# Two channel-weight pieces loaded behind the last pair's rows and staged where token sums will stand, in a one-core attention and token/channel-mixing kernel

## The chip, the core and the metric

The kernel runs on one core of one Trainium2 chip. The metric is the device time of one execution in microseconds (us). Three runs of the kernel before stand for it: 558.23, 559.42 and 561.3 us, median 559.42. The other figures come from one more execution, taken by the hardware profiler.

## What is computed

All data are float32. The reference first runs a decaying linear attention and then a token mixer and a channel mixer on its output:

```python
batch, n_heads, seq, head_dim = (4, 8, 768, 64)      # attention, in blocks of 64 rows
intra = (q k^T * Dmask) v                            # inside a block
inter = (q * lam_pow) kv_state                       # from the blocks before
x = attn_out.transpose(0, 2, 1, 3).reshape(4, 768, 512)
h = relu(x^T @ w_tok1) @ w_tok2                      # w_tok1 768x256, w_tok2 256x768
u = x + h^T
h2 = relu(u @ w_ch1) @ w_ch2                         # w_ch1 512x1536, w_ch2 1536x512
out = u + h2
```

## The kernel before

**Stages.** Attention works on 16 pairs of heads, `pairs[i] = (b, p)`, four pairs to each of the four batches. One loop over `i` from -2 to 15 (the first part of the span) computes the scores of pair i+1, the outputs of pair i, and between them pieces of the token mixer of batches already finished. The token pieces are taken from the list `groups`: `token_hidden` (18 matmuls of 256 columns into a tile `ph`, eighteen for each of four pieces of a batch) and `token_out` (6 matmuls of 384 columns into a tile `pu`, eight pieces of a batch). Batch 3's token outputs come behind the loop, in pairs of pieces. Then the channel mixer runs, in six groups of weights and four batches, with a seven-product scheme; it takes the rest of the span.

**The order is written by hand.** Each engine runs its queue in program order. The numbers in `take` say how many pieces of `groups` stage i runs, and `held` moves five of them: places 33 to 37 of the list become two hidden pieces of batch 3 (places 36 and 37) and then three output pieces of batch 2 (33 to 35). Stage 14 takes three pieces, stage 15 takes one, and four are left behind the loop. Smaller steps stand in `waiting`, and `later(n)` runs the next n of them between pieces.

**Loads.** `load_kq(i + 4)` at stage i loads a pair's rows: `kn`, four DMAs of 96 KB for `qn`, and from pair 8 on four of 96 KB for `kr` (L118). Runs of 32 numbers make their packets small. VectorE then turns `qn` and `kr` in blocks into `qT` (L255) and `kT` (L259), which the scores need. SP issues all of these loads in one queue.

**The first group's channel weights.** Their four raw pieces of 512 KB (i = 0 to 3 in `load_piece`) come in as 64-bit words. Each piece is narrowed to 32-bit floats by one step on ScalarE (L494) and four on VectorE (L495, L498, L501, L504), and then split into a high part (ScalarE, L486) and a low part (GpSimd, L487). All of that is staged in `w3`, which is the memory of batch 3's attention output, `uT[3]`. This has to be free before pair 12 writes there, so `later(99)` at stage 11 empties the list. Pieces 2 and 3 (`w_ch2` rows, L640) are issued by SP in stages 7 and 9, between the loads of pairs 11 and 12 and of pairs 13 and 14, and are narrowed in stages 10 and 11.

**Names.** `xp` is a transposed piece of the output of a pair (TensorE, L468); ScalarE rounds it to `xhi` (L475) and VectorE writes the rest, `xlo` (L476). `turn_back(i, 0)` and `turn_back(i, 1)` do this for the halves of pair i. L603 on VectorE adds a `pu` to `uT` and frees its bank; L565 and L566 finish a `ph`. L420 copies outputs from PSUM to `uT` (ScalarE). L333 masks scores and L303 scans states (VectorE); L316 and L282 are GpSimd's copies of states and its scaling of q. `first` holds steps that prepare batch 0's operands for the channel mixer (`t1` to `t4` are L698 and L731 on VectorE, `T1` to `T4` a cast L706 on ScalarE and a subtraction L711 on VectorE). `B11` and `B21` are two such operands whose low parts GpSimd makes.

**Banks.** `bank("sh", ...)` has three PSUM banks in turn and borrows the one of tag `xT` once a stage. The pieces `pu`, `ph` and `xp` all use them, so TensorE may be only three or four pieces ahead of what VectorE and ScalarE have emptied.

Of the kernel before, what the change touches and what calls it, by code (L numbers as in the profile page):

```python
# [13 lines left out]
U32 = mybir.dt.uint32  # L14
# [8 lines left out]
def kernel(  # L23
# [25 lines left out]
    DM = H * D  # L49
    FT = w_tok1.shape[1]  # L50
    FC = w_ch1.shape[1]
    P = 128
# [5 lines left out]
    SB = S // 2  # L58
# [5 lines left out]
    waiting = deque()  # L64

    def later(n):
        n += len(waiting) > (5 if len(groups) > 16 else 99)
        for _ in range(min(n, len(waiting))):
            waiting.popleft()()
# [6 lines left out]
    up = ctx.enter_context(tc.tile_pool(name="up", bufs=1))  # L76
# [14 lines left out]
    hidp = ctx.enter_context(tc.tile_pool(name="hidp", bufs=1, side="right"))  # L91
# [132 lines left out]
    n = 1  # L224
# [407 lines left out]
    def load_piece(g, i, raw):  # L632
        if i < 2:
            src = c1u[2 * i * P : 2 * (i + 1) * P, g * FG * 2 : (g + 1) * FG * 2]
            nc.sync.dma_start(
                out=raw.rearrange("p (t f) -> p t f", t=2), in_=src.rearrange("(t p) f -> p t f", p=P)
            )
        else:
            r0 = g * FG + (i - 2) * P
            nc.sync.dma_start(out=raw, in_=c2u[r0 : r0 + P, :])  # L640

    def narrow_piece(raw, a, sg):
        return narrow(raw.rearrange("p (n two) -> p n two", two=2), a, sg)
# [22 lines left out]
    def split_c2(to, i, a):  # L666
        c2h, c2l = to[4:]
        return lambda: split(c2h[:, i - 2], c2l[:, i - 2], a.bitcast(F32))
# [65 lines left out]
    weights = {}  # L734
# [10 lines left out]
    LATE = 7  # L745
    late_turns = deque([turn_q, turn_kr])
    idle = [lambda: None]
    held = [groups[n] for n in (36, 37, 33, 34, 35)]
    for n, f in enumerate(held):
        groups[33 + n] = f  # L750

# [1 line left out]
    for i in range(-2, NI):  # L755
        if 0 <= i + 1 < NI:
            pair = scores(i + 1)
            scale_q(i + 1)
        if i >= 0:
            outputs(i, 0)  # L760
        place = state(i + 1) if 0 <= i + 1 < NI else None
        if i + 1 in SCAN_FIRST:
            mask_scores(i + 1, 1, pair)
        work = [groups.popleft() for _ in range(take.get(i, 0))]
        if i == NI - 1:
            work.pop(0)()
        if i >= 0:
            outputs(i, 1)
            spare.append("xT")
        if i + 2 < NI and i != LATE:  # L770
            turn_q(i + 2)
            if i + 2 >= NKD:
                turn_kr(i + 2)
        if i + 2 < NI:
            if 0 < i + 2 < NP:
                masks(i + 2)
            turns = [(turn_k, 0), (turn_k, 1)] if i + 2 < NKD else []
            if i + 2 < NQ:
                turns += [(turn_q_rows, 0), (turn_q_rows, 1)]
            if i == -2:  # L780
                turns.sort(key=lambda x: x[1])
            for f, g in turns:
                f(i + 2, g)
        if place:
            place()
        later(0 if i == NI - 1 else 1 if work else 2)
        n = early.get(i, len(work) // 4)
        cuts = [0, n, max(n, (3 * len(work) + 1) // 4 if len(work) > 2 else len(work) // 2), len(work)]
        for n in range(3):
            for f in work[cuts[n] : cuts[n + 1]]:  # L790
                f()
                if i == LATE and n == 1 and late_turns:
                    late_turns.popleft()(i + 2)
                later(2 if len(work) < 3 else 1)
            if n < 2 and i >= 0:
                turn_back(i, n)
                later(1 if work else 2 + n)
            if n == 0 and i + 2 < NI:
                scale_k(i + 2)
                if i == LATE:  # L800
                    late_turns.popleft()(i + 2)
        if NSKIP - 4 <= i < NSKIP:
            own_blocks(i % 4)
        if NSKIP <= i + 2 < NI:
            load_firsts(i + 2)
        if i == -1:
            load_w1(0)
        if 0 <= i + 3 < NI and i >= -1:
            load_v(i + 3)
        if i == -1:  # L810
            load_w1(1)
        if i + 4 < NI:
            load_kq(i + 4)
        if i == -1:
            load_w1(2)
        if i == 3:
            load_w2()
        if 0 <= i < 3:
            convert_w1(i)
        if i == 5:  # L820
            weights[0] = group_tiles(0, False)
            w3 = words(3)
            load_piece(0, 0, w3[:, 2048:3072])
        if i == 4:
            steps = [w2_steps(n) for n in range(3)]
            waiting.extend(2 * idle + steps[0][:5] + idle + steps[0][5:] + steps[1][:2] + idle)
        if i == 5:
            waiting.extend(steps[1][2:5] + idle + steps[2][:2] + idle + steps[1][5:] + steps[2][2:] + idle)
        if i == 6:
            waiting.append(lambda: load_piece(0, 1, w3[:, 1024:2048]))  # L830
            steps = narrow_piece(w3[:, 2048:3072], w3[:, 0:512], w3[:, 512:1024])
            waiting.extend(idle + steps[:1] + 2 * idle + steps[1:2] + 2 * idle + steps[2:])
        if i == 7:
            steps = narrow_piece(w3[:, 1024:2048], w3[:, 512:1024], w3[:, 2048:2560])
            waiting.extend(3 * idle + steps)
            waiting.append(lambda: load_piece(0, 2, w3[:, 2048:3072]))
        if i == 8:
            waiting.extend(split_c1(weights[0], w3[:, 0:512], w3[:, 512:1024], nc.gpsimd))
        if i == 9:
            waiting.append(lambda: load_piece(0, 3, w3[:, 1024:2048]))  # L840
            waiting.extend(narrow_piece(w3[:, 2048:3072], w3[:, 0:512], w3[:, 512:1024]))
            waiting.append(split_c2(weights[0], 2, w3[:, 0:512]))
        if i == 10:
            homes[0] = {"B11": (up, None, 1), "B21": (up, None, 1), "T2": (kp, "kn", 2), "T1": (kp, "qn", 2)}
            homes[0] |= {"B22": (kp, "kr", 2), "T3": (kp, "kT", 2), "T4": (kp, "qT", 2)}
            first = build(0, 0, on_vector=("T1", "T2", "T3", "T4", "B22"))
            waiting.extend([first["B11"], first["B21"]])
            waiting.extend(narrow_piece(w3[:, 1024:2048], w3[:, 2048:2560], w3[:, 2560:3072]))
            waiting.append(split_c2(weights[0], 3, w3[:, 2048:2560]))
        if i == 11:  # L850
            later(99)
        if i == 13:
            for xs in (("t1",), ("t2", "T1.h"), ("T2.h", "T1.l"), ("T2.l", "t3", "t4"), ("T3.h", "T4.h"), ("T3.l", "T4.l")):
                waiting.append(lambda xs=xs: [first[x]() for x in xs])
    later(99)
    att.close()
    ch = ctx.enter_context(tc.tile_pool(name="ch", bufs=1, reuse_waits="tile"))
# [612 lines left out]
```

## Time and profile before

| | |
|---|---|
| runs: lowest, median, highest | 558.23, 559.42, 561.3 us |
| the profiled execution: its own time | 555.34 us |
| its span (first to last instruction) | 553.5 us |
| TensorE clock granted, share of full speed | 0.999 |
| busy share of TensorE, VectorE, ScalarE, GpSimd | 97%, 79%, 45%, 51% |
| bytes moved by DMA | 67.63 MB, mean 122 GB/s |
| loop over pairs with its token pieces | to about 166 us of the span |
| token outputs of batch 3 | 170.89 to 179.2 us |
| channel mixer | from 179.2 us |

The busy share of TensorE is a mean over stages; an idle interval shows only where a matmul starts later than the modelled end of the one before. Times inside the span are counted from its start. An interval of idle time in front of an instruction is given in square brackets in the timeline, with the engine and tile that ended it.

### The profile page before, as it was taken

The page shows a single profiled execution, that of the slowest core. Times are in us where ns is not written, and L with a number is a line of the kernel's source. Part 1 is how long each engine was busy: PE and PEld are TensorE (multiplying, and loading weights), DVE is VectorE, ACT ScalarE, POOL GpSimd, SP SyncE. Part 2 cuts the span into 40 slices and gives each one's busy share as a digit, 9 for nine tenths or more (in the row PEclk, how much of TensorE's full clock was granted, in tenths as well). Part 3 has the DMA queues.
Part 4 walks back from the last instruction along what each step waited for, and adds up shares of the span by engine and source line. Part 5 has one row for each costly group of instructions (what it writes and reads, how often), then busy time and mean ns, then how long its engine had stood idle before and what let it go on. Part 6 is the DMA issues. An engine that isn't in the chain of part 4 may idle for free.

```text
span 553.5 us, 11983 instructions
## 1 busy us (share of the span) xinstructions
PE 537.3 (97%) x4756; PEld 523.6 (95%) x4756; DVE 435.2 (79%) x657; ACT 247.4 (45%) x499; POOL 283.3 (51%) x260
## 2 busy tenths in 40 slices
PE   5999999979999999999999999999999999999997
PEld 4889999879889999999999999999999999999996
DVE  4787799668697989887878878788787878788894
ACT  3464543425252554343444443443455555445431
POOL 5667552737214464444435444354476656568550
PEclk9999999999999999999999999999999999999999
DMA  9999999999502534361725400014874131220276
GB/s 183 249 204 184 228 184 179 177 187 176 102 2 91 184 108 134 89 234 38 248 78 176 147 1 0 1 27 61 192 145 149 57 116 58 86 104 2 30 151 125
DMA packets 178760, 67.63 MB, mean 122 GB/s; under 512 B 166673, under 2 KB 168977, under 8 KB 178705
## 3 DMA queue, kind: packets, MB, share of 16 engines
q1 hardware_dynamic: 173472, 65.69, 49.5%
q10 hardware_dynamic: 5232, 1.18, 1.0%
q8 instruction: 37, 0.61, 0.4%
q14 instruction: 19, 0.15, 0.1%
HBM read 50.07 MB, written 16.78 MB: 121 GB/s over the span
## 4 chain that ended last, share of the span: by engine, by line
PE 81%; DMA 5%; SPq 5%; DVE 5%; ACT 1%; issue 1%; ACTq 0%; DVEq 0%
PE po L1149 22%; PE pa L923 13%; PE pc L923 9%; PE pb L923 7%; PE pa L1123 7%; PE pc L1123 5%; SPq L118 5%; DMA kr<-in_k_dram 3%; PE pd L923 3%; PE ph L561 2%; PE sc L371 2%; DMA qn<-in_q_dram 2%; PE pu L581 2%; PE xT L436 1%; PE pu L598 1%
## 5 line engine op out<-in xcount | busy, mean ns | idle before, releaser
L1162 DVE TENSOR_TENSOR uT<-po,uT 128x768 f32<-128x768 f32 x57 | 54.2, 952 | 16.5 <-PE po L1149 16.2
L938 ACT ACTIVATE c<-c 128x384 f32<-128x384 f32 x42 | 22.1, 526 | 58.5 <-DVE c L983 33.5
L316 POOL COPY stb<-sv 64x320 f32<-64x320 f32 x32 | 26.8, 839 | 35.1 <-DVE sv L303 34.1
L1129 DVE TENSOR_TENSOR uT<-pa,uT 128x768 f32<-128x768 f32 x36 | 34.4, 954 | 10.5 <-PE pa L1123 9.8
L940 POOL TENSOR_TENSOR h22l<-c,h22h 128x384 fp32r<-128x384 f32 x14 | 14.4, 1032 | 41.6 <-ACT h22h L939 41.6
L1129 DVE TENSOR_TENSOR uT<-pc,uT 128x768 f32<-128x768 f32 x27 | 25.8, 955 | 11.6 <-PE pc L1123 11.6
L487 POOL TENSOR_TENSOR c1l<-cs,c1h 128x512 fp32r<-128x512 f32 x15 | 19.3, 1296 | 23.2 <-ACT c1h L486 23.2
L333 DVE TENSOR_TENSOR a<-sc,mask 128x768 f32<-128x768 f32 (+1 forms) x32 | 25.9, 849 | 4.6 <-PE sc L371 4.1
L1149 PE MATMUL po<-h12h,c 128*128 128x384 f32 x112 | 28.7, 337 | 0.0
L1149 PE MATMUL po<-h11h,c 128*128 128x384 f32 x112 | 28.7, 337 | 0.0
L1149 PE MATMUL po<-h22h,c 128*128 128x384 f32 x112 | 28.6, 336 | 0.0
L1149 PE MATMUL po<-h21h,c 128*128 128x384 f32 x112 | 28.6, 336 | 0.0
L561 PE MATMUL ph<-xhi,w1h 128*128 128x256 f32 x96 | 28.2, 293 | 0.4 <-DVE uT L603 0.4
L561 PE MATMUL ph<-xhi,w1l 128*128 128x256 f32 x96 | 27.1, 283 | 0.0
L561 PE MATMUL ph<-xlo,w1h 128*128 128x256 f32 x96 | 27.1, 283 | 0.0
L282 POOL TENSOR_TENSOR qs<-qT,lamp 128x640 f32<-128x640 f32 x16 | 25.2, 1577 | 0.7 <-DVE qT L255 0.2
L476 DVE TENSOR_TENSOR xlo<-xp,xhi 128x384 fp32r<-128x384 f32 x32 | 17.7, 552 | 9.5 <-ACT xhi L475 9.4
L487 POOL TENSOR_TENSOR c<-cs,c 128x512 fp32r<-128x512 f32 x10 | 12.9, 1293 | 19.7 <-ACT c L486 19.7
L940 POOL TENSOR_TENSOR h21l<-c,h21h 128x384 fp32r<-128x384 f32 x14 | 17.7, 1262 | 8.8 <-POOL h22l L940 3.9
L940 POOL TENSOR_TENSOR h12l<-c,h12h 128x384 fp32r<-128x384 f32 x14 | 14.4, 1031 | 14.5 <-issue 10.4
L486 ACT CAST c1h<-cs 128x512 fp32r<-128x512 f32 x15 | 9.3, 617 | 26.7 <-DVE cs L660 18.9
L1149 PEld LDWEIGHTS po<-h12h,c 128*128 128x128 f32 x112 | 20.4, 188 | 0.0
(409 smaller groups left out, 2008.0 us busy)
## 6 DMA issues: line engine op xcount, KB each, us to landing
raw<-in_moe_w_ch_dram SPq DMA_DIRECT2D x20, 512.0 KB, 3.7
vn<-in_v_dram SPq DMA_DIRECT2D x16, 384.0 KB, 5.4
out_dram<-y SPq DMA_DIRECT2D x104, 48.0 KB, 1.9
qn<-in_q_dram SPq DMA_DIRECT2D x44, 96.0 KB, 3.6
kn<-in_k_dram SPq DMA_DIRECT2D x8, 384.0 KB, 6.6
kr<-in_k_dram SPq DMA_DIRECT2D x32, 96.0 KB, 3.1
dc1h<-c1h SPq DMA_DIRECT2D x4, 768.0 KB, 5.3
dc1l<-c1l SPq DMA_DIRECT2D x4, 768.0 KB, 6.7
```

Source lines behind the costliest of these rows:

```text
L118: nc.sync.dma_start(out=to[n * 32 : (n + 1) * 32].rearrange("p (blk d) -> p blk d", d=32), in_=sv[di])
L282: nc.gpsimd.tensor_mul(out=qss[i], in0=qTs[i][:, P:].rearrange("p (c i) -> p c i", i=P), in1=lamp[:, p, None, :].broadcast_to([P, NC - 1, P]),
L316: nc.gpsimd.tensor_copy(out=st[r, :, h, :], in_=sv[r].rearrange("p (e c) -> p c e", c=NC - 1))
L333: nc.vector.tensor_mul(out=a, in0=pair.rearrange("p h (c i) -> p h c i", i=w), in1=mask[:, 2 * p : 2 * p + 2, None, ms].broadcast_to([P, 2 ...
L487: nc.gpsimd.tensor_sub(out=lo, in0=src, in1=hi.bitcast(F32))
L561: nc.tensor.matmul(out=ph, lhsT=w[:, c, fs], rhs=x[:, c], start=(i == 0), stop=(i == 3 * NC - 1))
L923: nc.tensor.matmul(out=to, lhsT=w[:, t], rhs=x[:, t], start=(start and i == 0), stop=(i == 5), skip_group_check=not start,)
L940: nc.gpsimd.tensor_sub(out=hl, in0=src, in1=hh.bitcast(F32))
L1123: nc.tensor.matmul(out=pair[x][:, t], lhsT=w[:, t], rhs=h, start=(start and i == 0), stop=(i == 2), skip_group_check=not start,)
L1129: nc.vector.tensor_add(out=ub, in0=pair[x], in1=ub)
L1149: nc.tensor.matmul(out=to, lhsT=w[:, jj, t * P : (t + 1) * P], rhs=h, start=(i == 0), stop=(i == 3 * JG - 1))
L1162: nc.vector.tensor_add(out=ub, in0=po, in1=ub)
```

## The change

Pieces 2 and 3 are no longer loaded in stages 7 and 9 into `w3`. They go into a new tile `raw2`, in the place that the token sums (`hid`) of batches 1 and 3 share (tag `h1`), with `up`'s tiles for `B21` as temporaries. SP issues them in stages 11 and 12, the first behind the rows of pair 15. Their narrowing moves from stages 10 and 11 to stages 13 and 14; in stage 14 each step runs in front of a step of `first`. `B21` is prepared last, since its memory is the temporary. `held` is gone: the last pieces of `groups` are in their plain order, since batch 3's hidden pieces now need the memory of `raw2`.

```diff
     idle = [lambda: None]
-    held = [groups[n] for n in (36, 37, 33, 34, 35)]
-    for n, f in enumerate(held):
-        groups[33 + n] = f
+
+    def second_steps(n):
+        return narrow_piece(raw2[:, n], temp2[0], temp2[1]) + [split_c2(weights[0], n + 2, temp2[0])]
...
         if i == 7:
             steps = narrow_piece(w3[:, 1024:2048], w3[:, 512:1024], w3[:, 2048:2560])
             waiting.extend(3 * idle + steps)
-            waiting.append(lambda: load_piece(0, 2, w3[:, 2048:3072]))
...
-        if i == 9:
-            waiting.append(lambda: load_piece(0, 3, w3[:, 1024:2048]))
-            waiting.extend(narrow_piece(w3[:, 2048:3072], w3[:, 0:512], w3[:, 512:1024]))
-            waiting.append(split_c2(weights[0], 2, w3[:, 0:512]))
         if i == 10:
...
-            waiting.extend([first["B11"], first["B21"]])
-            waiting.extend(narrow_piece(w3[:, 1024:2048], w3[:, 2048:2560], w3[:, 2560:3072]))
-            waiting.append(split_c2(weights[0], 3, w3[:, 2048:2560]))
+            waiting.append(first["B11"])
         if i == 11:
             later(99)
+            raw2 = hidp.tile([P, 2, 1024], U32, tag="h1", name="raw2")
+            temp2 = [up.tile([P, 2 * SB], U32, tag=f"B21{x}0", name=f"temp2{x}")[:, 0:DM] for x in "hl"]
+        if i in (11, 12):
+            load_piece(0, i - 9, raw2[:, i - 11])
+        if i == 12:
+            waiting.extend(idle + second_steps(0))
         if i == 13:
-            for xs in (("t1",), ("t2", "T1.h"), ("T2.h", "T1.l"), ("T2.l", "t3", "t4"), ("T3.h", "T4.h"), ("T3.l", "T4.l")):
-                waiting.append(lambda xs=xs: [first[x]() for x in xs])
+            xss = (("t1",), ("t2", "T1.h"), ("T2.h", "T1.l"), ("T2.l", "t3", "t4"), ("T3.h", "T4.h"), ("T3.l", "T4.l"))
+            for f, xs in zip(second_steps(1), xss):
+                waiting.append(lambda f=f, xs=xs: [f()] + [first[x]() for x in xs])
+            waiting.append(first["B21"])
```

On SP's queue, the end of the loads in the loop. Before, from the rows of pair 14 on (`kr_1695` is pair 14's, `kr_2068` pair 15's):

```order
L118 DMA kr_1695<-in_k_dram 32x24x32 x4
L640 DMA uT_63<-in_moe_w_ch_dram 128x1024
L182 DMA vf_1866<-in_v_dram 64x6x64
...
L118 DMA kr_2068<-in_k_dram 32x24x32 x4
L182 DMA vf_2233<-in_v_dram 64x6x64
L168 DMA vn_2235<-in_v_dram 128x12x64
L182 DMA vf_2385<-in_v_dram 64x6x64
```

Now, from the rows of pair 15 on:

```order
L118 DMA kr_2048<-in_k_dram 32x24x32 x4
L640 DMA raw_2053<-in_moe_w_ch_dram 128x1024
L182 DMA vf_2217<-in_v_dram 64x6x64
L168 DMA vn_2219<-in_v_dram 128x12x64
L640 DMA raw_2053<-in_moe_w_ch_dram 128x1024
L182 DMA vf_2377<-in_v_dram 64x6x64
```

Both pieces now stand behind the last `kr`, and between them the v rows of pairs 14 and 15. The same holds for the earlier piece, which stood behind the `kr` of pair 11.

On ScalarE's queue in stage 13, before, from the copies of pair 13's outputs on:

```order
L420 COPY uT_63<-xT_2282 128x3x128
L475 CAST xhi_2174<-xp_2346 128x3x128
L275 ACTIVATE kd_2352<-kn_2061,mask 128x320 x2
L475 CAST xhi_2174<-xp_2371 128x3x128
L420 COPY uT_63<-xT_2431 128x3x128
```

Now:

```order
L420 COPY uT_63<-xT_2267 128x3x128
L494 ACTIVATE temp2h<-raw_2053 128x512
L475 CAST xhi_2158<-xp_2332 128x3x128
L275 ACTIVATE kd_2339<-kn_2041,mask 128x320 x2
L475 CAST xhi_2158<-xp_2360 128x3x128
L486 CAST c_1002<-temp2h 128x512
L420 COPY uT_63<-xT_2423 128x3x128
```

The first narrowing step, which needs the loaded piece, stands in front of the cast `xhi` of pair 13's first half.

On VectorE's queue in stage 14, before, from step `t2` on:

```order
L698 TENSOR_TENSOR tl_2494<-uT_60,th_2484 128x768
L603 TENSOR_TENSOR uT_62<-pu_2499,uT_62 128x384
L711 TENSOR_TENSOR T1l_2497<-th_2484,T1h_2496 128x768
L566 SCALAR_TENSOR_TENSOR h_2511<-ph_2512,h_2511 128x256
L711 TENSOR_TENSOR T2l_2508<-tl_2494,T2h_2507 128x768
L698 TENSOR_TENSOR th_2484<-uT_60 128x768
L731 TENSOR_TENSOR tl_2494<-uT_60,tl_2494 128x768
L476 TENSOR_TENSOR xlo_2487<-xp_2536,xhi_2486 128x3x128
L566 SCALAR_TENSOR_TENSOR h_2511<-ph_2548,h_2511 128x256
```

Now, from the narrowing step in front of `t2` on:

```order
L495 TENSOR_SCALAR temp2l<-raw_2053 128x512
L698 TENSOR_TENSOR tl_2488<-uT_60,th_2477 128x768
L603 TENSOR_TENSOR uT_62<-pu_2493,uT_62 128x384
L498 SCALAR_TENSOR_TENSOR temp2l<-raw_2053,temp2l 128x512
L711 TENSOR_TENSOR T1l_2491<-th_2477,T1h_2490 128x768
L603 TENSOR_TENSOR uT_62<-pu_2506,uT_62 128x384
L501 TENSOR_SCALAR temp2h<-temp2h 128x512
L711 TENSOR_TENSOR T2l_2503<-tl_2488,T2h_2502 128x768
L698 TENSOR_TENSOR th_2477<-uT_60 128x768
L731 TENSOR_TENSOR tl_2488<-uT_60,tl_2488 128x768
L476 TENSOR_TENSOR xlo_2480<-xp_2518,xhi_2479 128x3x128
L504 SCALAR_TENSOR_TENSOR temp2h<-temp2h,temp2l 128x512
```

Four narrowing steps came in, three of them in front of the second `xlo` of pair 14, and two additions of `pu` (L603) stand where two hidden pieces were finished (L566). On TensorE the two hidden pieces of batch 3 that ran in stage 14 now run behind the loop, ahead of the other two, and three output pieces of batch 2 run in stages 14 and 15 that ran in stage 15 and behind the loop.

## Rows read from the trace of the kernel before

**Rows 1.** The page: busy share of each engine, and DMA in 40 slices.

```profile
PE 537.3 (97%) x4756; PEld 523.6 (95%) x4756; DVE 435.2 (79%) x657; ACT 247.4 (45%) x499; POOL 283.3 (51%) x260
...
DMA  9999999999502534361725400014874131220276
```

**Rows 2.** Busy time: stretch, length, PE, PEld, DVE, ACT, POOL, PEclk, DMA share, GB/s.

```profile
120.00:138.20 18.20, 18.20 (x404) 17.53 (x404) 15.16 (x23) 9.23 (x20) 13.98 (x11) 1.00 1.01 186
138.20:148.90 10.70, 9.64 (x196) 8.57 (x194) 7.02 (x11) 3.22 (x7) 3.23 (x4) 1.00 0.76 134
148.90:161.00 12.10, 11.81 (x254) 11.13 (x254) 10.45 (x14) 5.03 (x9) 2.24 (x2) 1.00 0.01 3
```

**Rows 3.** Timeline of TensorE in stage 10: start, us, instruction, idle before it.

```profile
116.79 0.61 PE L598 MATMUL pu<-w2h,h 128*128 128x384 f32 x2 [2.77 <-DVE xlo L476]
...
118.66 0.62 PE L598 MATMUL pu<-w2h,h 128*128 128x384 f32 x2 [0.22 <-DVE uT L603]
```

**Rows 4.** Timeline of VectorE in stage 10.

```profile
114.52 0.98 DVE L259 STREAM_TRANSPOSE kT<-kr 128x768 f32<-128x768 f32 x1 [3.73 <-DMA kr<-in_k_dram]
...
115.86 0.41 DVE L495 TENSOR_SCALAR uT<-uT 128x512 uint32<-128x512 uint32 x1
116.19 0.55 DVE L476 TENSOR_TENSOR xlo<-xp,xhi 128x384 fp32r<-128x384 f32 x1
116.66 0.68 DVE L498 SCALAR_TENSOR_TENSOR uT<-uT 128x512 uint32<-128x512 uint32 x1
```

**Rows 5.** Timeline of SP: piece 2, and the last row loads of pair 15.

```profile
97.74 1.43 SPq L640 DMA_DIRECT2D uT<-in_moe_w_ch_dram  x1
...
139.96 3.08 SPq L118 DMA_DIRECT2D kr<-in_k_dram  x3
```

**Rows 6.** DMA view, 100 to 102.2 us, then 105 to 135 us.

```profile
DMA packets 670, 0.62 MB, mean 280 GB/s; under 512 B 552, under 2 KB 552, under 8 KB 670
...
q1 hardware_dynamic: 670, 0.62, 95.4%
...
DMA packets 27031, 5.01 MB, mean 167 GB/s; under 512 B 26897, under 2 KB 26897, under 8 KB 27025
...
q1 hardware_dynamic: 27025, 4.92, 93.1%
```

**Rows 7.** A later stretch in which weights are saved and loaded, columns as in rows 2.

```profile
190.00:196.00 6.00, 6.00 (x36) 6.00 (x35) 5.73 (x7) 1.74 (x3) 3.54 (x3) 1.00 1.04 425
```

**Rows 8.** Issue to landing: L640 in the loop, then later pieces (the page's median).

```profile
DMA to landing us min/median/max: 4.8/5.0/5.2
...
raw<-in_moe_w_ch_dram SPq DMA_DIRECT2D x20, 512.0 KB, 3.7
```

**Rows 9.** Timeline of stage 13: VectorE, ScalarE, TensorE.

```profile
145.20 0.98 DVE L259 STREAM_TRANSPOSE kT<-kr 128x768 f32<-128x768 f32 x1 [1.16 <-DMA kr<-in_k_dram]
...
147.73 0.48 ACT L475 CAST xhi<-xp 128x384 fp32r<-128x384 f32 x1 [2.30 <-PE xp L468]
...
147.15 0.55 PE L468 MATMUL xp<-ident,uT 128*128 128x128 f32 x3 [1.05 <-DVE xlo L476]
```

**Rows 10.** Timeline: a narrowing step on ScalarE, then VectorE steps in stages 11 and 14.

```profile
126.32 0.70 ACT L494 ACTIVATE uT<-uT 128x512 f32<-128x512 f32 x1
...
128.57 1.59 DVE L498 SCALAR_TENSOR_TENSOR uT<-uT 128x512 uint32<-128x512 uint32 x1
...
154.51 1.59 DVE L698 TENSOR_TENSOR tl<-uT,th 128x768 f32<-128x768 f32 x1
...
158.55 0.95 DVE L698 TENSOR_TENSOR th<-uT 128x768 f32<-128x768 f32 x1
```

**Rows 11.** The chain that ended last, end of the loop: start, us, what.

```profile
160.89 1.32 PE pu L598 x6
...
164.49 2.09 PE pu L598 x12
166.58 4.31 PE ph L561 x36
```

## The prediction

> **What bounds the kernel now.** The page comes first: TensorE is busy 97% of the span, and DMA is full for the first ten slices, to about 140 us, and seldom after [rows 1]. So the loop over pairs has two masters. Stretch by stretch [rows 2], TensorE is busy for all of 120 to 138.2 us while DMA is full too; from 138.2 to 148.9 us it misses 1.1 us, and from 148.9 to 161 us 0.3 us, with VectorE busy 10.45 of 12.1 us there and DMA at rest. Then the timeline says where TensorE stands idle and for whom. The largest interval is in stage 10: 2.77 us, ended by an `xlo` on VectorE [rows 3]. VectorE had itself waited 3.73 us for the `kr` of pair 12, and a narrowing step of a channel piece stood between the turn of `kr` and that `xlo` [rows 4]. The next idle is in stage 13: 1.05 us, again for an `xlo`, behind a turn that waited 1.16 us for the last `kr` [rows 9]. Behind the loop TensorE is full to the end of the span, so what the loop loses or wins is the whole effect.
>
> **The price of a moved load.** Piece 2 is issued at 97.74 us [rows 5], ahead of pair 12's rows. From 100 to 102.2 us the queue holds 95.4% of the DMA engines, 2.10 us in all, for 118 packets of 512 B or more (670 less 552) and 552 smaller ones. From 105 to 135 us, 93.1% of 30 us, 27.9 us, went nearly all to 26,897 small packets: 1.04 ns each [rows 6]. The 552 took 0.57 us, so the 118 took 1.53 us, and the piece's 128 take 1.66; I use 1.7 us. The ends: 512 KB at 425 GB/s, a stretch in which weights move, is 1.23 us [rows 7]; at 186 GB/s, the mixed rate of the full queue, it is 2.8 us [rows 2]. The Trainium skill (DMA: Bandwidth & Descriptors, Specifications) puts the fabric's ceiling at 435 GB/s; by it a piece takes an estimated 1.2 us and the sum below would end near +3.5 us. The rows show that rate only where large packets run alone, so I stay with 1.7.
>
> **Stage 10: a gain of 2.2 us.** Without piece 2, pair 12's `kr` lands 1.7 us earlier. L495 between the turn and the `xlo` goes: 0.33 us from its start to the next [rows 4]. The 2.77 us of idle shrink by 2.03. The addition that ended the 0.22 us [rows 3] stood behind L498, which is gone too. Together 2.2 us; the ends are 1.8 (with 1.23 for the piece) and 3.0 (all of both). The eight VectorE steps that leave stages 10 and 11 free no more, since TensorE had no idle left up to 138.2 us [rows 2]. TensorE thus comes to stage 13 2.2 us earlier.
>
> **Stage 13: half of that is given back.** The last `kr` has two pieces fewer ahead of it, 3.4 us, so its turn can start at 141.8 instead of 145.20. TensorE reaches the transposes that waited at 146.1 - 2.2 = 143.9 us [rows 9]. But now ScalarE's first narrowing step (L494) stands in front of the cast `xhi` whose `xlo` they wait for, and it needs piece 2. SP issues that when the last `kr` is issued, 143.04 - 3.4 = 139.6 us [rows 5]. L640 landed 4.8 to 5.2 us after its issue in the full queue, and later pieces 3.7 us after theirs [rows 8]; this queue is emptying (DMA share 0.76 [rows 2]), so I take 4.3: 143.9 us. Then L494 0.70 [rows 10], the cast 0.48 [rows 9] and `xlo` 0.55 [rows 4]: 145.7 us with small hand-overs, against 147.15. A step L495 in front of the next addition costs 0.3 more before the scores of pair 15. So 1.1 us remain. The landing's ends, 143.3 and 144.8, leave 1.7 and 0.2. Behind the waiting L494 on ScalarE stand both casts of pair 13 and the scaling of k; VectorE waits for the casts, and TensorE for the banks.
>
> **Stage 14: VectorE's queue sets the pace.** ScalarE's second L494 stands ahead of `xhi`: 0.6 later (0.70 less an overlap of 0.1), so 0.5 early. L495 costs 0.33. `t2`, which took 1.59 us beside GpSimd's state copy, comes after that copy now and takes 0.95 like its neighbours [rows 10]: 0.64 won, 0.8 early. Ahead of the second `xlo` come L498 (0.68, about 0.6 from start to start) and L501 (0.33), and an addition in place of a shorter finishing step, 0.13: about 0.3 late. That `xlo` frees the bank of the `pu` that started at 160.89 us [rows 11]; it starts 0.3 us late.
>
> **Behind it: 2.2 us of work that had run earlier.** From that `pu` on, TensorE ran three pieces of output and two of hidden, 2.09 us for two outputs and 4.31 for two hidden [rows 11]. Now all four hidden pieces and no further output stand there: 4.31 - 2.09 = 2.2 us more. The same 2.2 us are missing ahead of that `pu`, where TensorE waits for VectorE. No step of the channel mixer makes up for it.
>
> **Costed at nothing.** The v rows of pairs 14 and 15 stand behind piece 2 on SP, 1.7 us, but move up 3.4. GpSimd's subtraction for piece 2 stands in front of pair 15's scaling, which is needed some 8 us later. The cast for piece 3 on ScalarE stands ahead of pair 15's copies; TensorE runs the `pu` meanwhile. `B21` is made at the loop's end, more than 15 us before its product. If these covers fail, each costs under 1 us.
>
> **The sum** is 0.3 + 2.2 = +2.5 us: 555.34 + 2.5 = 557.8 for the profiled execution, which lay 4.1 us under the median of the runs; on that median, 559.42 + 2.5 = **561.9 us**. With the pieces at 2.8 us the load is in before TensorE asks in stage 13, which gives 1.8 back: +0.7. With the late landing, or the pieces at 1.23, +3.4; with `t2` still slow, +4.0. So +0.7 to +4.0 for this case. A measurement of this kernel can tell about 0.5%, 2.8 us, from no change.
>
> **Rivals.**
> *Faster: the last pairs hide the steps.* If the second `xlo` of pair 14 is done before TensorE asks for its bank, the order of the pieces costs nothing; the 2.2 and the 1.05 us of idle are won: 556.2 us. With less work ahead, TensorE asks at about 160.89 - 3.2 - 2.2 = 155.5 us, so VectorE must be 5.7 us quicker than in my walk. It has 1.65 us idle in that stretch [rows 2] against two narrowing passes of some 1.9 us each in the last two stages. The relief by DMA speaks for it.
> *Much slower: the narrowing meets GpSimd.* An L498 beside GpSimd's work took 1.59 us, not 0.68 [rows 10]. Two such steps in stage 14 add 1.8 us: +4.3, 563.7 us. It decides if GpSimd's state copy or its piece subtraction overlaps them. The Trainium skill (GPSIMD Engine Reference, Specifications) says that GpSimd shares its SBUF interfaces with VectorE and contends with instructions of two SBUF inputs, which L498 has; the rows agree.
> *The pieces were not in the way.* If `kr` comes no earlier, stage 10 wins 0.55 and piece 2 lands 4.3 us after 143.04, at 147.3, so stage 13 ends some 2 us late instead of 1.1 early: near +5.6, 565 us. The full queue speaks against it.
> *Level.* A relief of 2.8 us a piece and an early landing: -1 to +0.7, about 559.3 us.
>
> **Chances.** Forecast 0.50 (0.35 of it at or under 2.8 us, 0.15 above), faster rival 0.12, GpSimd 0.17, no relief 0.06, level 0.15. So faster by over 0.5%: 0.12; within: 0.35 + 0.15 = 0.50; slower: 0.15 + 0.17 + 0.06 = 0.38. The faster rival and the one without relief are left out of the range; the rest runs from -1.0 to +4.6, and I add 0.5 at the lower end for the spread of the runs: 557.9 to 564.0.
>
> **What would show it.** In the new profile: the idle near 116.8 us under 1 us; the turn of pair 15's `kr` near 142; L494 on ScalarE waiting for a DMA in stage 13, and TensorE idle there for 1.5 to 2 us; in stages 14 and 15 three intervals of TensorE idle for VectorE, 4 us or more together; four `ph` in a row behind the loop. No idle in stage 14 would make me wrong on the side of a gain; an unchanged 2.77 us, on the other.

## The result, and the profile after

The changed kernel takes 563.11 us in the median of 22 runs (559.48 to 565.29), the kernel before on the same chip 559.37 (22 runs). The ratio is 1.0071, 95% interval 1.0049 to 1.0093: **slower by 0.7%, 4.0 us** (2.7 to 5.2). The forecast was +2.5 us, with +4.0 as the end of its own case. The time lies in the range, but the change is beyond the 0.5% within which I had put half of the chance. The ratio is taken from the runs, not from the two medians, so a difference worked out from it need not be theirs.

The profiled execution of the changed kernel took 562.18 us (span 560.4, granted clock 0.991), 6.84 us more than that of the kernel before. The first experiment shows why this pair of traces differs by more than the medians.

The page of the changed kernel. The DMA row is full for nine slices, where [rows 1] have ten; the clock has a dip in the eleventh slice.

```profile
PE 540.1 (96%) x4756; PEld 526.0 (94%) x4756; DVE 433.5 (77%) x657; ACT 248.2 (44%) x499; POOL 284.1 (51%) x260
...
PEclk9999999999799999999999999999999999999999
DMA  9999999997501254172534410004775122130176
```

The stretches of [rows 2] and the one behind them, same columns:

```profile
120.00:138.20 18.20, 18.20 (x405) 17.45 (x403) 11.36 (x18) 7.61 (x17) 7.95 (x7) 1.00 0.86 155
138.20:148.90 10.70, 5.61 (x29) 4.95 (x28) 4.90 (x9) 2.90 (x6) 1.54 (x2) 0.81 0.85 200
148.90:161.00 12.10, 10.63 (x200) 9.30 (x203) 9.47 (x16) 4.47 (x8) 5.06 (x4) 0.88 0.02 4
161.00:168.00 7.00, 5.10 (x71) 4.10 (x68) 6.46 (x10) 2.81 (x5) 2.41 (x1) 0.81 0.12 32
```

From 138.2 to 148.9 us TensorE is busy for 5.6 us, where it had 9.6 before, and in all three stretches behind 138.2 the granted clock is below 1.00. What TensorE waited for from 70 to 260 us (us in all, times, longest):

```profile
PE xp L468 <- DVE xlo L476: 5.1, 1, 5.1
PE pu L598 <- DVE xlo L476: 1.9, 1, 1.9
PE pu L598 <- DVE uT L603: 1.7, 2, 1.1
```

The 2.77 us of stage 10 [rows 3] are gone, and 5.1 us in stage 13 have come. The timeline there, of TensorE, ScalarE, VectorE and SP:

```profile
147.01 0.90 PE L468 MATMUL xp<-ident,uT 128*128 128x128 f32 x3 [5.09 <-DVE xlo L476]
...
145.34 0.66 ACT L494 ACTIVATE temp2h<-raw 128x512 f32<-128x512 f32 x1 [6.55 <-DMA raw<-in_moe_w_ch_dram]
145.90 0.46 ACT L475 CAST xhi<-xp 128x384 fp32r<-128x384 f32 x1
...
143.31 0.98 DVE L259 STREAM_TRANSPOSE kT<-kr 128x768 f32<-128x768 f32 x1 [2.36 <-DMA kr<-in_k_dram]
...
140.34 1.58 SPq L640 DMA_DIRECT2D raw<-in_moe_w_ch_dram  x1
```

ScalarE's L494 waited 6.55 us for piece 2, which landed 5.0 us after its issue, and `xhi` stood behind it; the turn of the last `kr` had been done at 144.3. The granted clock around this wait (stretch, length, busy time of TensorE, PEclk, DMA share, GB/s):

```profile
142.00:144.00 2.00, 0.00 (x0) 1.00 0.70 206
144.00:146.00 2.00, 0.00 (x0) 0.71 0.95 238
146.00:148.00 2.00, 0.99 (x4) 0.50 1.06 297
148.00:150.00 2.00, 2.00 (x6) 0.50 0.32 88
150.00:152.00 2.00, 2.00 (x85) 0.58 0.00 0
...
166.00:168.00 2.00, 2.00 (x23) 0.50 0.39 105
```

At 0.50 TensorE runs at 1.2 GHz instead of 2.4. That happens twice: the clock falls while TensorE still waits in stage 13, and again behind the three waits of stages 14 and 15:

```profile
158.91 0.44 PE L598 MATMUL pu<-w2h,hh 128*128 128x384 f32 x1 [1.11 <-DVE uT L603]
160.84 0.27 PE L392 MATMUL xT<-a,vf 64*64 64x64 f32 x2 [0.36 <-DVE uT L603]
164.25 0.45 PE L598 MATMUL pu<-w2h,hh 128*128 128x384 f32 x1 [1.90 <-DVE xlo L476]
```

The end of the loop in the chain of waits, to be held against [rows 11]:

```profile
164.25 1.44 PE pu L598 x6
...
169.09 8.64 PE ph L561 x72
177.73 8.33 PE pu L581 x48
```

The `pu` in stage 15's place, which started at 160.89 us, starts at 164.25 (it is now piece 35 of `groups`, called f35 below), four `ph` stand in a row, and the first output of batch 3 comes at 177.73 instead of 170.89. From there to the end both spans have 382.6 to 382.7 us left: the whole difference arises in the loop.

### The profile page after: what moved, and what is told of

Read it like the earlier page. It is cut to its first block, busy times and chain, and to the rows that moved or that the text cites. A ratio compares the mean times of both kernels' runs of the same rounds, so it can differ in the third digit from the quotient of the medians.

```text
span 560.4 us, 11982 instructions
## 1 busy us (share of the span) xinstructions
PE 540.1 (96%) x4756; PEld 526.0 (94%) x4756; DVE 433.5 (77%) x657; ACT 248.2 (44%) x499; POOL 284.1 (51%) x260
## 4 chain that ended last, share of the span: by engine, by line
PE 88%; DMA 4%; DVE 3%; SPq 2%; issue 1%; ACT 1%; ACTq 0%; DVEq 0%
PE po L1150 21%; PE pa L924 12%; PE pc L924 9%; PE pb L924 7%; PE pa L1124 7%; PE ph L561 5%; PE pc L1124 5%; PE pu L598 3%; PE pd L924 3%; DMA qn<-in_q_dram 2%; PE xp L468 2%; PE sc L371 2%; PE sc L354 2%; PE xT L413 2%; PE pu L581 1%; SPq L118 1%
## 5 line engine op out<-in xcount | busy, mean ns | idle before, releaser
L468 PE MATMUL xp<-ident,uT 128*128 128x128 f32 x96 | 16.5, 290 | 5.2 <-DVE xlo L476 5.1
```

What stands on the lines that cost most here:

```text
L468: nc.tensor.transpose(out=xp[:, c * P : (c + 1) * P], in_=chunks_of(uT[b][:, p], i, g)[:, c], identity=ident)
```

## Experiments

Ratios are to runs of the kernel before made on the same chip beside the run's own, with 95% intervals; the microseconds are worked out from the ratio. e3, e6 and e12 leave weights out, so only their times count.

| run | ratio | us against before |
|---|---|---|
| e3: no loads of the two pieces | 0.9891 (0.9851 to 0.9931) | -6.1 |
| e11: piece 2 alone behind the loop | 0.9969 (0.9947 to 0.9992) | -1.7 |
| e12: as changed, no narrowing of the two | 0.9978 (0.9945 to 1.0012) | -1.2 |
| e6: as changed, no loads of the two | 0.9991 (0.9962 to 1.0020) | -0.5 |
| e9: both pieces behind the loop, in free memory | 0.9995 (0.9965 to 1.0025) | -0.3 |
| e5: both behind the loop, in the token sums' place | 1.0011 (0.9982 to 1.0041) | +0.6 |
| e8: as e5, steps spread | 1.0019 (0.9991 to 1.0047) | +1.1 |
| e10: as e9, steps in another order | 1.0031 (1.0004 to 1.0058) | +1.7 |
| e1: as changed, narrowing later | 1.0037 (1.0012 to 1.0063) | +2.1 |
| e2: plain order alone | 1.0053 (1.0024 to 1.0082) | +3.0 |
| the change | 1.0071 (1.0049 to 1.0093) | +4.0 |
| e4: as changed, one output piece computed four times | 1.0073 (1.0047 to 1.0098) | +4.1 |

**e0: the kernel before, once more.**

> The kernel before, unchanged, profiled once more. The profiled execution that the prediction used lay 4 us under the median of its runs and had a granted clock of 0.999.
> Theory G (that execution was an early one, and a usual one loses more to late rows): with a time near 560 us the turn of pair 12's kr comes after 114.5 us, that of pair 15 after 146 us, TensorE's idle time in stages 10 and 13 is 6 us or more in all (3.8 in the first profile), and the granted clock is below 1.00 behind one of these intervals.
> Rival (the spread of the times is made elsewhere, in the channel mixer or at the start): stages 10 and 13 look as in the first profile.

This execution took 562.82 us, 1.7 over the median of the runs of this kernel beside it. Its stretches (columns as in [rows 2]) and two turns of `kr`:

```profile
104.20:120.00 15.80, 11.73 (x203) 10.46 (x201) 9.04 (x17) 4.46 (x10) 8.03 (x9) 1.00 0.95 168
...
148.90:161.00 12.10, 8.66 (x179) 7.60 (x178) 6.79 (x11) 1.59 (x5) 1.63 (x2) 0.86 0.26 54
...
116.27 0.98 DVE L259 STREAM_TRANSPOSE kT<-kr 128x768 f32<-128x768 f32 x1 [2.60 <-DMA kr<-in_k_dram]
...
151.21 0.98 DVE L259 STREAM_TRANSPOSE kT<-kr 128x768 f32<-128x768 f32 x1 [2.96 <-DMA kr<-in_k_dram]
```

Theory G holds. The last `kr` is turned 6 us later than in [rows 9], TensorE waits 2.79 us in stage 10 and 3.44 in stage 13, and the clock halves behind the second wait in the kernel before too. The trace of the prediction was one in which the rows came early. The granted clocks say that some half clock is the usual case, though not where: of 110 runs of the kernel before that stand beside the experiments, one has 0.999 like the first trace, all others less, with a median of 0.994.

**e3: without the two loads.**

```diff
-            waiting.append(lambda: load_piece(0, 2, w3[:, 2048:3072]))
...
-            waiting.append(lambda: load_piece(0, 3, w3[:, 1024:2048]))
```

> The kernel before without the loads of pieces 2 and 3 (left out of the computation: these weights; the narrowing runs on the old contents of the same memory). Every other instruction stays.
> Theory A (the relief is real, 1.7 us or more for each piece): the turn of pair 12's kr comes some 2 us earlier and that of pair 15 some 3.5 us earlier than in the kernel before, and the time falls by 2.5 to 5 us, to 555.5 to 558 us.
> Rival (the queue of small packets sets the rows' landing, whatever large packets stand between): within 1 us of the kernel before.

555.52 us against 561.17: -6.1 us (-3.9 to -8.4). In its profile:

```profile
111.10 0.98 DVE L259 STREAM_TRANSPOSE kT<-kr 128x768 f32<-128x768 f32 x1 [0.35 <-DMA kr<-in_k_dram]
...
142.57 0.98 DVE L259 STREAM_TRANSPOSE kT<-kr 128x768 f32<-128x768 f32 x1 [1.31 <-DMA kr<-in_k_dram]
```

The relief is real, and in time nearly twice what I priced: 3.0 us a piece, not 1.7. Not all of it is the queue's: e3's six runs have granted clocks of 0.997 to 1.000, the runs of the kernel before beside them 0.988 to 0.997, so the 6.1 us hold some half clock that most of e3's runs no longer have. The rows themselves say less, and roughly, since they scatter by some 5 us: pair 12's `kr` is turned at 115.7 us in the mean with piece 2 ahead of it (three profiles), at 113 without it (eleven); pair 15's at 149.0 with both ahead (three), at 144.3 without (ten). That is 2.7 us for one piece and 4.7 for two.

**e2: the plain order alone.**

```diff
-    held = [groups[n] for n in (36, 37, 33, 34, 35)]
-    for n, f in enumerate(held):
-        groups[33 + n] = f
```

> The kernel before with the last groups in their plain order, and nothing else changed: the pieces are loaded and narrowed where they were.
> Theory B (the order costs): 2.2 us of hidden pieces move behind the loop and leave TensorE waiting for VectorE in stages 14 and 15, so +1.5 to +2.5 us against the kernel before, 561 to 562 us.
> Theory A (the wait in stage 13 costs, the order is nearly free while no narrowing stands in stages 14 and 15): within 0.8 us of the kernel before, no idle over 0.6 us in stages 14 and 15.

+3.0 us (1.3 to 4.6). One of TensorE's waits from 70 to 260 us, and a stretch of the clock (columns as in the table of the change's clock above):

```profile
PE pu L598 <- DVE xlo L476: 4.2, 2, 2.6
...
168.00:170.00 2.00, 1.86 (x6) 0.61 0.05 12
```

Stage 10's 2.63 us and a wait of 3.45 in stage 13 are as in e0. New is a wait of 1.57 us in front of f35, and the clock falls behind it. Theory B holds, with somewhat more than its 1.5 to 2.5 us: the order costs this without any narrowing in stages 14 and 15.

**e6 and e12: the changed kernel without the loads, and without the steps.** e6 takes away what L494 waits for:

```diff
-            load_piece(0, i - 9, raw2[:, i - 11])
+            nc.gpsimd.memset(raw2[:, i - 11], 0)
```

> The changed kernel without the loads of pieces 2 and 3 (left out of the computation: GpSimd writes zeros into their place in stages 11 and 12 instead). The order of the groups and all narrowing steps stay, and L494 in stage 13 waits for no DMA.
> Theory A (the wait for the landing of piece 2 and the clock behind it cost most): TensorE's idle time in stage 13 falls to under 2.5 us, and the time falls by 3 to 5 us against the changed kernel, to 558.5 to 560.5 us, no longer slower than the kernel before.
> Theory B (the order of the groups costs most): it falls by less than 2 us and stays 1.5 us or more above the kernel before.

-0.5 us against before, so 0.8% or 4.5 us under the changed kernel (the intervals leave about 2 us either way). Stage 13 has 10.45 us of work in 10.7:

```profile
138.20:148.90 10.70, 10.45 (x262) 9.41 (x261) 8.60 (x15) 3.70 (x8) 1.59 (x2) 1.00 0.66 119
148.90:161.00 12.10, 9.06 (x172) 7.85 (x163) 11.68 (x17) 5.21 (x9) 5.15 (x4) 1.00 0.01 1
161.00:168.00 7.00, 6.32 (x50) 5.60 (x51) 4.97 (x9) 4.06 (x8) 3.39 (x2) 0.76 0.48 152
```

Theory A holds for the wait, though the edit takes away more than that: no piece stands on SP ahead of the v rows either, and in this trace TensorE was held up for 1.58 us in stage 10. But 5.6 us of the relief are still missing, and the two rows behind show where: VectorE busy 11.68 of 12.1 us, TensorE 9.06, and the clock low again after it. e12 leaves out the narrowing steps and keeps the loads:

```diff
-        return narrow_piece(raw2[:, n], temp2[0], temp2[1]) + [split_c2(weights[0], n + 2, temp2[0])]
+        return 5 * idle + [split_c2(weights[0], n + 2, uT[0][:, 0, 0:DM])]
```

> The changed kernel without the narrowing steps L494, L495, L498, L501 and L504 of pieces 2 and 3 (left out of the computation: these weights; the split that follows reads another tile instead). The loads stay where the change put them, nothing in the loop waits for them, and the order of the groups stays as changed.
> So far: the relief is worth 6.1 us, the order costs 3.0, and a version without the loads but with order and steps lies 0.5 us under the kernel before.
> Theory A+B (the order costs some 3 us and the ten steps in stages 13 and 14 the 2.6 that are left): the kernel comes out at the relief less the order, 3 us under the kernel before, -0.4 to -0.8%, and f35's output piece starts 1.5 us or more ahead of its time in the version without loads (about 161.7 us).
> Rival (the order costs all 5.6 us of it, the steps nothing): within 0.25% of the kernel before.

-1.2 us (-3.1 to +0.7): between the two theories, and f35 started at 161.46 us, only 0.2 ahead of e6. So my split into 3.0 for the order and 2.6 for the steps doesn't hold. The steps are worth 0.7 us by these two runs, which can't be told from nothing; e6 also lacks the loads that e12 has. e12 lies 4.9 us above e3, more than the 3.0 of e2, but that is not the order alone. Its profile has 1.57 us of idle in front of f35 and 3.50 in stage 13, where e3 has 1.23, and a low clock behind both. The idle of stage 13 is for the last `kr`:

```profile
143.95 0.98 DVE L259 STREAM_TRANSPOSE kT<-kr 128x768 f32<-128x768 f32 x1 [2.77 <-DMA kr<-in_k_dram]
145.89 0.90 PE L468 MATMUL xp<-ident,uT 128*128 128x128 f32 x3 [3.50 <-DVE xlo L476]
```

How the 5.6 us divide between order and steps stays open within some 2.5 us.

**e1: the steps moved behind the wait.**

```diff
-            waiting.extend(idle + second_steps(0))
+            waiting.extend(5 * idle + second_steps(0))
...
+                waiting.extend(2 * idle if n == 2 else [])
```

> The changed kernel, with the narrowing of piece 2 begun five places later, so that L494 stands on ScalarE behind the casts of both halves of pair 13, and with the last four steps of piece 3 and of the operands behind the transposes of pair 15. Loads and order of the groups stay as changed.
> Theory A (the wait of L494 for piece 2 is what costs): the 5.1 us of idle TensorE in stage 13 shrink to 1 us or less, the granted clock stays at 1.00 from 138 to 152 us, and the time falls by 4 to 7 us, to 556 to 559 us, at or below the kernel before.
> Theory B (the order of the last groups and VectorE's load in stages 14 and 15 cost): stage 13 gets faster, but what it wins returns as idle time in stages 14 and 15, since the same steps are now crowded there, and the time falls by less than 2 us: above 561 us.
> Theory C (the last kr or the v rows are the bound in stage 13): the idle of stage 13 stays above 3 us, now in front of another instruction.

+2.1 us against before, some 1.9 better than the change (the two intervals overlap): theory A promised twice that. The L494 wait is gone, but 3.53 us of idle remain in stage 13, in front of the same transposes, behind the turn of the last `kr`: there theory C is what happened.

```profile
144.33 0.98 DVE L259 STREAM_TRANSPOSE kT<-kr 128x768 f32<-128x768 f32 x1 [3.63 <-DMA kr<-in_k_dram]
146.27 0.85 PE L468 MATMUL xp<-ident,uT 128*128 128x128 f32 x3 [3.53 <-DVE xlo L476]
```

And the steps that moved now stand in front of the `ph` behind the loop:

```profile
PE ph L561 <- DVE h L566: 4.2, 1, 4.2
PE xp L468 <- DVE xlo L476: 3.8, 2, 3.5
```

**e4: TensorE kept busy in the wait.** The third output piece of stage 13 is computed four times.

```diff
+        for _ in range(again.pop() if again else 1):
...
+                if i == 13 and f is work[2]:
+                    again.append(4)
```

> The changed kernel, in which the output piece that stands in front of the wait of stage 13 is computed four times over into the same bank, with the same result, so that TensorE is busy for 3.7 us of the 5.1 in which it stood idle.
> Theory D (the granted clock fell because TensorE had stood idle, and the half speed behind it costs time): the clock stays at 1.00 from 147 to 152 us, the pieces there take 1.3 us and not 2.3, and though 18 matmuls are added the time falls by 1.5 to 3 us, to 560 to 561.6 us.
> Rival (the clock has no part in it, or falls for another reason): the clock is at 0.5 again behind the wait, or the speed won there is lost in the next wait for VectorE: within 0.8 us of the changed kernel, 562.3 to 564 us.

No gain: theory D fell as a way to win time. The rows came later in this execution, and 1.66 us of idle remained. The clock fell all the same:

```profile
146.00:148.00 2.00, 1.76 (x11) 1.00 0.91 273
148.00:150.00 2.00, 0.55 (x3) 1.00 1.19 293
150.00:152.00 2.00, 1.78 (x18) 0.79 0.49 152
152.00:154.00 2.00, 2.00 (x86) 0.50 0.00 0
```

So it doesn't tell what the half clock costs when it is avoided; that is read from rows only (below).

**e5, e8, e9, e10, e11: the pieces behind the loop.** With the old order kept, pieces are loaded and narrowed after the last pair. e5 and e8 put both ahead of the second group's pieces (e8 with the steps spread), e9 and e10 into memory that the attention leaves free; e10 changes the order of the steps, and e11 moves piece 2 alone. The cut shown is e11's:

```diff
+    raw2 = ch.tile([P, 1024], U32, name="raw2")
+    temp2 = [ch.tile([P, 2 * SB], U32, tag=f"T3{x}1", name=f"temp2{x}")[:, 0:DM] for x in "hl"]
+    p2 = [*narrow_piece(raw2, *temp2), split_c2(weights[0], 2, temp2[0])]
+    load_piece(0, 2, raw2)
-    order = [[first["B22"]], [parts["B11"]], [parts["t1"]], [parts["t2"], parts["B21"]]]
+    order = [[first["B22"]], [parts["B11"]], [*p2[:5], parts["t1"]], [parts["t2"], parts["B21"], p2[5]]]
```

> The kernel before, with its own order of the last groups, in which pieces 2 and 3 are loaded behind the loop, in the place of batch 2's token sums, ahead of the pieces of the second group, and narrowed beside the last token outputs; the second group's pieces 0 to 2 come some 8 us later.
> Theory A (the relief of the loads in the loop is real, and only the places of the wait, the order and the steps spoil it): the idle of stages 10 and 13 goes as in the changed kernel or better, with nothing given back in the loop, so the loop ends 4 to 5 us earlier and the time is 554 to 556 us.
> Theory E (the relief is given back whatever the place, since the loop ends on VectorE or on the last rows): the loop ends less than 2 us earlier and the time is 557.5 us or more.
> Theory F (the steps are late now for the channel mixer): new idle of TensorE for VectorE, ScalarE or a DMA between 178 and 230 us that eats 2 us or more.

> The kernel with pieces 2 and 3 loaded and narrowed behind the loop (own order of the last groups), now with the steps spread: piece 2 beside the last token outputs, piece 3 in the first unit of the channel mixer, piece 0 of the second group at the end of that unit, its piece 1 in the next.
> Theory A (the relief in the loop is worth 4 us or more, and the first version behind the loop lost it to 3.9 us of idle time at 180.6 us, where a cast for piece 3 stood in front of a copy of the first products): that idle goes, and the time falls to 555 to 558 us, 0.5% or more under the kernel before.
> Theory F (VectorE is too full behind the loop whatever the places): new idle of TensorE of 2 us or more between 178 and 230 us, and the time is within 1.5 us of the kernel before.

> The kernel before, with its own order of the last groups, in which pieces 2 and 3 are loaded one after the other behind the loop into memory that the attention leaves free, so that nothing of the second group moves. Their steps stand between the last hidden and output pieces of the token mixer (166 to 178 us), and the first steps of the second group come one output piece later.
> Theory A (the relief in the loop is worth about 6 us, as leaving the loads out showed, and the two versions behind the loop gave it back because piece 2 landed only near 170 us and VectorE was too full between 178 and 200 us): the first output piece L581 starts at 168 to 171 us, no idle of TensorE over 1 us stands behind it, the span is L581's start plus 383 us, and the time is 553.5 to 557.5 us, 0.7 to 1.3% under the kernel before.
> Theory F (the steps cost the same wherever TensorE depends on VectorE): TensorE waits 2 us or more for VectorE or ScalarE between 166 and 200 us, and the time is within 0.4% of the kernel before.

> As the version before it (both pieces one after the other behind the loop, own order of the last groups), with the narrowing put where GpSimd rests: piece 2 ahead of the operand B21, piece 3 between B21 and the splits, the operand T1 last; the second group's piece 0 goes into the first unit of the channel mixer and its piece 1 into the next.
> Theory A with the lesson of that version (its steps L501 and L495 took 2.07 us instead of 0.42, ending 0.3 us behind a GpSimd operation each time): all ten steps take under 0.8 us, TensorE's idle time behind L581's start falls from 3.8 to under 1.5 us, and the time is 554.5 to 558 us, 0.5 to 1.2% under the kernel before.
> Theory F (VectorE has no room for two more pieces in 166 to 205 us): 2 us or more of idle for VectorE remain, and the time is within 0.4% of the kernel before.

> The kernel before with piece 2 alone loaded and narrowed behind the loop (ahead of B21), piece 3 left where it was, the order of the groups and everything of the second group unchanged.
> Theory A (a piece ahead of the rows costs 3 us, as leaving both out showed 6): the rows of pairs 12 to 15 land 3 us earlier, VectorE has room for one piece (it is busy 6.4 of 10 us from 168 to 178 us), and the time falls by 2 to 3.5 us, 0.35 to 0.6% under the kernel before.
> Theory F (any narrowing behind the loop is given back): within 0.2% of the kernel before.

All four versions with both pieces come out between -0.3 and +1.7 us. In e5, e8 and e9 the loop ends early, as theory A says: the first matmul of L581 comes at 170.0, 170.0 and 170.4 us. The early first trace of before has it at 170.7, e0 at 178.2. But from there their spans take 388.6 to 388.7 us, not the 382.8 of both traces of before: some 6 us are given back, as theory F says. In e9 the waits behind 170 us are 1.31, 1.66 and 0.78 us, and the clock is 0.86 from 178 to 190. For the first of them, which an addition ends that VectorE starts only at 174.99 us, a cause stands in the rows of VectorE and GpSimd:

```profile
172.28 2.07 DVE L501 TENSOR_SCALAR temp2h<-temp2h 128x512 f32<-128x512 f32 x1
...
177.83 2.07 DVE L495 TENSOR_SCALAR temp2l<-raw 128x512 uint32<-128x512 uint32 x1
...
171.74 2.33 POOL L711 TENSOR_TENSOR B21l<-uT,B21h 128x768 fp32r<-128x768 f32 x1 [3.40 <-ACT B21h L706]
...
177.28 2.34 POOL L711 TENSOR_TENSOR T1l<-th,T1h 128x768 fp32r<-128x768 f32 x1 [0.18 <-ACT T1h L706]
```

Each of these VectorE steps, 0.42 us elsewhere, lasts until 0.28 us after the GpSimd operation beside it. e10 kept most steps clear of GpSimd (one still took 1.51 us) and still waited 4.5 us behind L581's start, the longest 1.87 us for VectorE at 205 us. So GpSimd is not the whole cause. That VectorE has no room for two more pieces there fits all four but isn't shown; only these four orders were tried. e11, with one piece, has a single wait of 0.98 us behind the loop and is faster than the kernel before: 559.85 against 561.56 us, ratio 0.9969 (0.9947 to 0.9992), somewhat less than the 2 to 3.5 us of its theory.

## Why the prediction was right in size and where its steps failed

The direction and the range held; the terms held less well, and it took some luck: relief and losses were both priced too low, and the errors cancelled in part. The prediction also gives no working for the +4.6 at the upper end of its range. In order of its steps:

- **The price of a moved load** was mis-sized: 1.7 us by the packets' share of the engines' time; 3.0 by e3 with the clock in it, 2.3 to 2.7 by the rows of all profiles. Both are near the upper end, 2.8, which I had from the mixed rate of the full queue [rows 2] and set aside. By the sentence on the Trainium skill (DMA: Bandwidth & Descriptors, Specifications) a piece would take an estimated 1.2 us; the measurements decide for more here, where small packets fill the queue.
- **Stage 10** was right in kind: the idle of 2.77 and 0.22 us is gone. The scores of pair 12 start 4.2 us earlier (115.70 instead of 119.90), 3.8 of it won between the scores of pairs 11 and 12, where I took 2.2: pair 12's `kr` was turned 4.6 us earlier (109.91 instead of 114.52), where I took 1.7.
- **Stage 13** is the step that failed: "1.1 us remain". The wait was the one I named, L494 in front of `xhi`. But piece 2 was issued 0.7 us later than I took, needed 5.0 us to land instead of 4.3, and the transposes restarted at 147.01 instead of 145.7: against 147.15 before, nothing remained. Behind both stands the last `kr`, which I took to move by 3.4 us, to 141.8; it was turned at 143.31. Without the wait for piece 2 the transposes follow the start of this turn by 1.95 us (145.20 to 147.15 before, 1.94 in e1 and e12), so they would have started at 145.26. The wait for piece 2 thus cost 1.75 us of the 5.09, about the 1.8 of idle that I had forecast; the other 3.3 are for the last `kr`, because TensorE came earlier than forecast and the rows did not.
- **What the step left out** is the clock. Between that restart and the `pu` of stage 15 (now f35) the trace has 17.24 us, 13.74 before: 3.5 us more. 1.45 of it is VectorE's longer way from `t1` to the second `xlo` of pair 14 (154.75 to 163.65 us, 7.45 before); the other 2.05 lie ahead of `t1`, where the transposes, a `pu` and the scores took 5.03 us at half clock instead of 2.99 (the `pu` from its start on 2.28 instead of 1.31).
- **Stage 14** held: from "1.1 early" to "0.3 late" I had added 1.4 us, and VectorE's way got 1.45 longer. `t2` took 0.95 and both L498 0.68, so the rival with GpSimd did not happen in this kernel, though the sum it named, 563.7 us, was near.
- **Behind it** the chain has 13.48 us from that `pu` to L581, 10.00 before [rows 11]: the 2.2 us of moved work, and 1.3 more at half clock.
- **The sum.** In the pair of traces: -0.14 + 3.50 + 3.48 = 6.84 us, of which about 3.4 are half clock by the two differences above, the rest the 2.5 that I had summed plus the 1.0 of stage 13 that did not remain. Over all runs it is 4.0. The traces of e0 and e2, whose loads stand as before, have a long wait and a half clock in stage 13 as well, so a usual run of the kernel before has less to lose there. I had noted that the profiled execution lay 4 us under the median and moved the sum by that, without asking which of its waits were short for that reason.

**The rivals.** "The pieces were not in the way" is refuted by e3. "The last pairs hide the steps" is refuted by the waits in stages 14 and 15. "Level" needed 2.8 us a piece, which came about true, and an early landing of piece 2, which did not. Of the signs, the idle of stage 10 and the four `ph` came as forecast; the three intervals of stages 14 and 15 make 3.4 us, not 4 or more, and the idle of stage 13 was 5.1, not 1.5 to 2.

**The balance that the runs give:** relief -6.1 (e3), order +4.9 (e12 against e3), steps +0.7 (e6 against e12), the wait for piece 2 with its clock +4.5 (the change against e6): +4.0. The four add up by construction, each has an interval of 2 to 3 us to either side, and the last three compare ratios that were not taken side by side. The terms are not pure either. The 4.9 holds the longer wait for the last `kr` in e12; e2 alone puts the order at 3.0. The 4.5 holds more than the wait for piece 2: the rows of stage 13 give that 1.75 us, e1, which takes it away, won some 1.9 while its moved steps cost a wait of 4.17 behind the loop, and at f35 e6 is 2.6 us ahead (161.68 against 164.25). So the relief and a cost of the order are shown; how the losses divide is not.

## What to carry to other kernels

Price a load taken out of a full queue at the queue's own mixed rate: here the rows came 2.3 to 2.7 us earlier for each piece, and the two together were worth 6 us of time. The gain was lost in more than one place. The new order of the pieces left TensorE waiting for VectorE, and the first step that reads the late load stood in the queue of an engine ahead of the cast that TensorE needed. Put such a step behind everything that the bounding engine waits for, keep the order of pieces that covers VectorE, and ask what the bounding engine meets when it arrives earlier: here it was the next rows. And profile the kernel before twice: here an execution 4 us under the median had shorter waits than the usual one.

## What the runs showed of the hardware

- **The half clock follows a wait, but not every wait.** It came with 5.09 us of idle (the change), 3.44 (e0), 3.5 (e12), but also with 1.66 us in e4 and, in stage 10, with 1.80 in e5 and 2.15 in e9; and not with 2.77 us in the first trace of the kernel before [rows 3]. All traces in plain order but e1 and e4 show it near f35 (0.81 in the change, 0.76 in e6 and e12, from 161 to 168 us; 0.61 in e2 from 168 to 170); none in the held order does. The longest single wait just before was 1.90 us in the change and e6 and 1.57 in e2 and e12; in e4 one of 1.90 us had no fall behind it.
- **Some of VectorE's steps are held up by GpSimd**, as above: 2.07 us instead of 0.42, ending 0.28 us after GpSimd's operation. Which steps meet it changed with the order: in e10 it was an L698 (2.27 us instead of 0.95, beside `B21`). The Trainium skill (Trainium Architecture — The Big Picture, What this means for kernel authors) says of the port pair that the two share that "it's an exclusive lock (not a bandwidth split)". The rows of e9 agree.
